# Attention into a token and channel mixer on one core: the order of the first batch, and where transposes find their PSUM banks

## The chip, the cores and the metric

The kernel runs on one NeuronCore of a Trainium2 chip. A core has engines that run side by side, each with its own queue, worked in order: TensorE (PE, matrix products, with its weight loads shown apart as PEld), VectorE (DVE), ScalarE (ACT) and GpSimd (POOL), and SyncE (SP), which here only issues transfers. Matrix products land in PSUM, from which VectorE and ScalarE copy results to SBUF. The metric is the device time of one execution in microseconds. Before the change the median of 6 runs is 382.45 us, from 381.56 to 384.02.

## The reference

Attention with squared ReLU in place of softmax, for 8 batch entries, 12 heads, 448 positions and 64 columns a head; then a mixer over tokens and one over channels:

```python
scores = scale * np.matmul(q, k.transpose(0, 1, 3, 2))
attn = np.maximum(scores, 0.0) ** 2 / S
x = np.matmul(attn, v)             # heads side by side: (8, 448, 768)
h = np.maximum(xt @ w_tok1, 0.0) @ w_tok2          # xt: x with tokens last
u = x + h.transpose(0, 2, 1)
h2 = np.maximum(u @ w_ch1, 0.0) @ w_ch2
out = u + h2
```

The token weights are 448 x 256 and 256 x 448, the channel weights 768 x 1536 and 1536 x 768. Inputs and output are float32; the kernel computes in bfloat16 with float32 sums.

## The kernel before

**Groups.** The 96 heads are worked in 24 groups of four heads; three groups make up one batch entry. A group goes through these steps, each a Python function that appends instructions to the engines' queues.

- `load_four(i)` (L73) loads q, k and v of four heads, two transfers for each tensor, on POOL's queue. They turn float32 into bfloat16 on the way. Only k of group 0 comes over the SP and ScalarE queues as float32 and is cast. Each POOL transfer also waits for the transfer eight places before it, since eight semaphores go round.
- `transposes(i)` (L128): 56 small PE transposes put q and k with the head dimension on the partitions, in two halves r; each half is one PSUM bank (128 x 896 bfloat16) and is copied to the SBUF tile `qkT` (L152).
- `scores(i, c)` (L157): seven tiles c of a group. Four products into a pair of banks, then ReLU on ScalarE (L172) into a tile `at`. `square` (L176) squares finished tiles on VectorE and can keep the last one back.
- `values(i, cs)` (L181) multiplies the tiles with v and sums into `acc_ps`, two banks; `values_out` (L200) scales both halves into `xT`, on VectorE, or with `split` the second half on ScalarE.
- `x_back` (L222) transposes x for the token product: for the first six groups on PE, into one bank, with a copy to `x_sb`; later by transfers on SP's queue.
- `token1` (L252) is the first token product, with ReLU on ScalarE (L265) into `r_sb`; `token2` (L268) is the second; its two halves `h_ps` are added to `xT` into `uT_sb` on VectorE (L289). `u_back` then sends u back transposed through SP's queue.
- `channel1` (L315): one unit is six products of 128 x 448 and a ReLU, 12 units a batch entry. `channel2` (L353): twelve products of 128 x 384 and an addition.

**PSUM.** The pool `ps_att` has two pairs of banks, which the score tiles take in turn; `ps_acc` has one pair, for `acc_ps` and several others; `ps_mm` has two single banks, taken in turn. The 8 banks are all given away. A tile of a pool can be written again once every reader of the tile before it in that place is done. The framework finds all waits from the tiles that instructions read and write.

**Order.** The order is written out by hand, in three stretches. The first (L439 to L464) is a loop over groups 0 to 2 and, in each, over the seven score tiles; the work of the group before (its last three value tiles, its token products) is put between them. The second (L467 to L495) is group 3 written out, with the first channel products (`channel1_begin` and `channel1_end`, which split two units so that the last third of u can come late). The third (L497 on) is a loop over the other groups. In it `fill(share)` takes channel units from a queue: each call adds a share of `rate` to a credit, and units are taken while the credit is positive, or at least `least` of them.

In the first two stretches the transposes are called with `early=True`: each half takes a bank of `ps_mm` of its own, and ScalarE copies half 0, VectorE half 1. The same banks serve `x_back`, `token1` and `token2`. The transposes of group i+1 are put behind score tile 3 of group i. In the third stretch they use the pair of `ps_acc`, and VectorE copies both halves.

Of the kernel before, what the change touches and what calls it, by code (L numbers as in the profile page):

```python
# [9 lines left out]
FP32 = mybir.dt.float32  # L10
BF16 = mybir.dt.bfloat16
# [5 lines left out]
def kernel(  # L17
# [52 lines left out]

    raws = {}
    k_first = consts.tile([128, 2, QC, D], FP32, name="k_first")
    def load_four(i):  # L73
        b, d = divmod(i, DB)
        tiles = []
        for name, src in (("q", q), ("k", k), ("v", v)):
            t = raw.tile([128, 2, QC, D], BF16, name=f"{name}_raw")
            for r in range(2):
                h0 = 4 * d + 2 * r
                eng, dst = nc.gpsimd, t  # L80
                if i == 0 and name == "k":
                    eng, dst = (nc.sync, nc.scalar)[r], k_first
                eng.dma_start(  # L83
                    out=dst[64 * r : 64 * (r + 1)].rearrange("p g c d -> p g (c d)"),
                    in_=src[b, h0 : h0 + 2].rearrange("g (p c) d -> p g (c d)", c=QC),
                )
            if i == 0 and name == "k":
                nc.scalar.copy(t[:, 0], k_first[:, 0])
                nc.vector.tensor_copy(t[:, 1], k_first[:, 1])
            tiles.append(t)  # L90
        raws[i] = tiles

    def load_wt1():
        w = moe_w_tok1.rearrange("(p c) j -> c p j", c=QC)
# [30 lines left out]

    qkT, at2, squares, accs = {}, {}, [], {}

    def transposes(i, early=False):  # L128
        sb = attn.tile([128, 2, 2, S], BF16, name="qkT")
        if early:  # L130
            parts = [ps_mm.tile([128, 1024], BF16, tag="bank", name="qkT_ps1") for r in range(2)]
        else:
            both = ps_acc.tile([128, 2, 1024], BF16, tag="acc", name="qkT_ps")
            parts = [both[:, r] for r in range(2)]
        for w in (1, 0) if i == 0 else (0, 1):
            src = raws[i][w]
            for c in range(QC):
                at = w * S + c * 64
                for r in range(2):
                    h = slice(64 * r, 64 * (r + 1))  # L140
                    for g in range(2):
                        nc.tensor.matmul(  # L142
                            parts[r][64 * g : 64 * (g + 1), at : at + 64],
                            lhsT=src[h, g, c, :],
                            rhs=ident[h, h],
                            is_transpose=True,
                            start=True,
                            stop=True,
                            skip_group_check=True,
                        )  # L150
        for r in range(2):
            (nc.scalar.copy if early and r == 0 else nc.vector.tensor_copy)(  # L152
                sb[:, r].rearrange("n w t -> n (w t)"), parts[r][:, : 2 * S]
            )
        qkT[i] = sb

# [22 lines left out]
            nc.vector.tensor_tensor(out=at, in0=at, in1=at, op=ALU.mult)  # L179

    def values(i, cs):  # L181
        v_raw = raws[i][2]
        if i not in accs:
            accs[i] = ps_acc.tile([128, 2, 512], FP32, tag="acc", name="acc_ps")
        ps = accs[i]
        for c in cs:
            at = at2.pop((i, c))
            for r in range(2):
                for g in range(2):
                    h = slice(64 * r, 64 * (r + 1))  # L190
                    nc.tensor.matmul(  # L191
                        ps[64 * g : 64 * (g + 1), r, :S],
                        lhsT=v_raw[h, g, c, :],
                        rhs=at[h, g, :],
                        start=(c == 0),
                        stop=(c == QC - 1),
                        skip_group_check=True,
                    )

    def values_out(i, split=False):  # L200
        b, d = divmod(i, DB)
        ps = accs.pop(i)
        raws.pop(i)
        for r in range(2):
            if split and r == 1:
                nc.scalar.activation(
# [13 lines left out]
    XDMA = 6  # L220
# [44 lines left out]
        nc.scalar.activation(r1, ps, AF.Relu)  # L265
        r1_tiles[i] = r1

    def token2(i, early=False):  # L268
        b, d = divmod(i, DB)
        if d == 0 and b % 2 == 0:  # L270
            uT_tiles[b // 2] = mix.tile([128, NP, 2 * S], BF16, name="uT_sb")
        r1 = r1_tiles.pop(i)
        off = (b % 2) * S
        if early:
            parts = [ps_mm.tile([128, 512], FP32, tag="bank", name="h_ps1") for r in range(2)]
        else:
            both = ps_acc.tile([128, 2, 512], FP32, tag="acc", name="h_ps")
            parts = [both[:, r] for r in range(2)]
        for r in range(2):
            for j in range(JC):  # L280
                nc.tensor.matmul(  # L281
                    parts[r][:, :S],
                    lhsT=r1[:, j, r * 128 : (r + 1) * 128],
                    rhs=wt2[:, j, :],
                    start=(j == 0),
                    stop=(j == JC - 1),
                )
        for r in range(2):
            nc.vector.tensor_tensor(  # L289
                out=uT_tiles[b // 2][:, 2 * d + r, off : off + S],  # L290
                in0=parts[r][:, :S],
                in1=xT[b % 2][:, 2 * d + r, :S],
                op=ALU.add,
            )
        u_back(i)


    r2_tiles, u_tiles, out_tiles = {}, {}, {}
# [127 lines left out]
        nc.vector.memset(xT[i][:, :, S:], 0.0)  # L426
    nc.vector.memset(wt1[:, 3, :], 0.0)
    make_identity(nc, ident)
    load_four(0)
    load_four(1)  # L430
    load_wt1()
    load_four(2)
    load_wt2()
    load_four(3)
    load_wc1(0, 2)
    order_wt2()


    transposes(0, early=True)  # L439
    for i in range(DB):  # L440
        for c in range(QC):
            scores(i, c)
            square(keep=1)
            if c < 3 and i > 0:
                values(i - 1, (4 + c,))
                if c == 2:
                    values_out(i - 1)
            if c == 0 and i > 1:
                token2(i - 2, early=True)
            if c == 3:  # L450
                transposes(i + 1, early=True)
            if c == 4 and i > 0:
                x_back(i - 1)
            if c == 5:
                values(i, (0, 1))
            if c == 6:
                if i > 0:
                    token1(i - 1)
                values(i, (2, 3))
        if i == 1:  # L460
            load_four(4)
# [12 lines left out]
    scores(i, 1)  # L474
    token1(i - 1)
    square(keep=1)
    first = channel1_begin()
    scores(i, 2)
    token2(i - 1, early=True)
    square(keep=1)  # L480
    channel1_end(first)
    scores(i, 3)
    transposes(i + 1, early=True)
    square(keep=1)
    scores(i, 4)
    channel_work(0)
    queue.pop(0)[1]()
    square(keep=1)
    scores(i, 5)
    scores(i, 6)  # L490
    square(keep=1)
    queue.pop(0)[1]()
# [3 lines left out]

    rate[0] = len(queue) * C1 / DB  # L497
    for i in range(DB + 1, ND + 2):
        if i == 2 * DB + 1:
            rate[0] = (EC * C1 + NT * C2) / DB  # L500
        if i < ND:
# [4 lines left out]
            values_out(i - 1)  # L506
        if i < ND:
            scores(i, 2)
        if i - 1 < XDMA:
            fill(1 / 3, least=1)  # L510
        if 0 <= i - 1 < ND:
            x_back(i - 1)
# [4 lines left out]
        if i == 4:  # L517
            load_wc2(1, 2)
        square()
        if i - 1 >= XDMA:  # L520
            fill(1 / 3)
        if i < ND:
            scores(i, 3)
# [1 line left out]
        if i + 1 < ND:  # L525
            transposes(i + 1)
        square()
        fill(2 / 9)
        if 0 <= i - 1 < ND:
            token1(i - 1)  # L530
        fill(1 / 9, least=1)
        if i < ND:
            scores(i, 5)
            scores(i, 6)
# [38 lines left out]
```

## Time and profile before

| quantity | value |
|---|---|
| median of 6 runs | 382.45 us (381.56 to 384.02) |
| the profiled execution | 381.56 us, span 379.8 us |
| PE busy | 363.1 us, 96% of the span |
| VectorE busy | 205.5 us, 54% |
| ScalarE busy | 213.9 us, 56% |
| GpSimd busy | 98.3 us, 26% |
| PE busy from 0 to 10 us, 10 to 20, 20 to 30, 30 to 40 | 6.42, 7.18, 7.95, 8.27 us |
| ReLU of one score tile (L172) | 0.92 us, 168 times |
| square of one tile (L179) | 0.63 us, 168 times |
| mean granted TensorE clock | 0.999 |

The span is the time from the first to the last instruction of the profiled execution. "Busy" is the time in which an engine has an instruction at work. In a view of waits, a line names the engine and line that waited, what it waited for, the total, the number of times and the longest wait, all in us. In the timeline a line has the start, the length, the engine, the line, the operation, output and input, the count, and in brackets the idle time before it with what ended it. A strip cuts the span in 40 slices, with the busy share of each in tenths.

### The profile page before, as it was taken

What the parts mean: (1) busy time and instruction counts of PE and PEld (TensorE: products, weight loads), DVE (VectorE), ACT (ScalarE), POOL (GpSimd) and SP (SyncE); (2) the same over time, 40 slices, a digit from 0 to 9 for tenths busy, and PEclk for the clock granted to TensorE, in tenths of its full rate; (3) what the DMA queues carried; (4) which work ended last, traced back from release to release, by engine and by line L of the source; (5) the groups of instructions that cost most, each with busy time, mean ns of one, the idle gap of its engine ahead of it and who ended that gap; (6) DMA issues with size and microseconds to landing.
All of it is one profiled execution on the core that took longest, in us unless ns stands there. A gap on an engine that the chain in (4) does not pass through costs nothing.

```text
span 379.8 us, 10027 instructions
## 1 busy us (share of the span) xinstructions
PE 363.1 (96%) x4281; PEld 200.0 (53%) x4281; DVE 205.5 (54%) x373; ACT 213.9 (56%) x297; POOL 98.3 (26%) x176
## 2 busy tenths in 40 slices
PE   6768899999999999999999999999999999999995
PEld 2444455554565555555555655555545654555563
DVE  1795577864486575465555665556654755121022
ACT  3985887867545447754676247654676455411400
POOL 9976244330412303303303303313300000000000
PEclk9999999999999999999999999999999999999999
DMA  8999999974658868648746688498551343223024
GB/s 155 128 198 179 191 203 190 167 99 73 92 140 148 164 117 135 99 70 157 128 76 93 115 169 145 44 115 157 116 84 24 83 109 87 42 65 89 2 56 110
DMA packets 72013, 43.82 MB, mean 115 GB/s; under 512 B 46048, under 2 KB 68512, under 8 KB 71968
## 3 DMA queue, kind: packets, MB, share of 16 engines
q0 software_dynamic: 24416, 21.47, 39.5%
q1 hardware_dynamic: 47248, 21.28, 28.0%
q8 instruction: 33, 0.54, 0.6%
q10 hardware_dynamic: 304, 0.43, 0.4%
q14 instruction: 12, 0.10, 0.1%
HBM read 43.38 MB, written 11.01 MB: 143 GB/s over the span
## 4 chain that ended last, share of the span: by engine, by line
PE 87%; ACT 5%; DVE 4%; issue 2%; DMA 1%; POOL 0%; POOLq 0%; ACTq 0%
PE m_ps L361 29%; PE m_ps L322 28%; PE sc_ps L163 9%; PE acc_ps L191 8%; PE t_ps L257 5%; PE h_ps L281 4%; ACT at L172 4%; PE qkT_ps L142 2%; DVE at L179 2%; DMA q_raw<-in_q_dram 1%; PE x_ps L235 1%; DVE uT_sb L289 1%; ACT qkT L152 1%; PE m_ps L340 1%; DVE qkT L152 1%
## 5 line engine op out<-in xcount | busy, mean ns | idle before, releaser
L172 ACT ACTIVATE at<-sc_ps 128x896 bf16<-128x896 f32 x168 | 144.9, 923 | 60.3 <-PE sc_ps L163 60.3
L322 PE MATMUL m_ps<-uT_sb,wc 128*128 128x448 bf16 x564 | 115.3, 353 | 0.7 <-DVE qkT L152 0.7
L361 PE MATMUL m_ps<-wc,r_sb 128*128 128x384 bf16 x672 | 115.2, 326 | 0.0
L179 DVE TENSOR_TENSOR at<-at 128x896 bf16<-128x896 bf16 x168 | 98.0, 625 | 6.3 <-ACT at L172 6.2
L361 PEld LDWEIGHTS <-r_sb 128*128 128x128 bf16 x672 | 64.3, 98 | 45.8 <-issue 4.1
L329 ACT ACTIVATE r_sb<-m_ps 128x448 bf16<-128x448 f32 x94 | 51.3, 545 | 58.8 <-PE m_ps L322 58.3
L322 PEld LDWEIGHTS <-wc 128*128 128x128 bf16 x564 | 53.2, 98 | 50.2 <-issue 5.0
L368 DVE TENSOR_TENSOR out_sb<-m_ps,u_sb 128x384 f32<-128x384 f32 x56 | 31.1, 556 | 58.8 <-PE m_ps L361 58.8
L163 PE MATMUL sc_ps<-qkT 64*64 64x448 bf16 x672 | 54.0, 368 | 5.0 <-ACT at L172 3.6
L289 DVE TENSOR_TENSOR uT_sb<-h_ps,xT 128x448 bf16<-128x448 f32 x48 | 27.7, 620 | 50.5 <-PE h_ps L281 50.4
L210 DVE TENSOR_SCALAR xT<-acc_ps 128x448 bf16<-128x448 f32 x47 | 27.2, 620 | 29.1 <-PE acc_ps L191 29.1
L515 POOL COPY gate<-x_sb 1x1 bf16<-1x1 bf16 x14 | 3.4, 242 | 145.2 <-DMA x_sb<-xT 145.2
L191 PE MATMUL acc_ps<-at,v_raw 64*64 64x448 bf16 x672 | 38.3, 353 | 0.1
L83 POOL DMA_DIRECT2D q_raw<-in_q_dram x48 | 28.9, 611 | 27.1 <-DMA wc<-in_moe_w_ch_dram 23.1
L152 DVE COPY qkT<-qkT_ps 128x896 bf16<-128x896 bf16 x43 | 25.1, 620 | 19.3 <-PE qkT_ps L142 18.0
L163 PEld LDWEIGHTS <-qkT 64*64 64x64 bf16 x672 | 16.2, 106 | 33.6 <-issue 29.7
L83 POOL DMA_DIRECT2D v_raw<-in_v_dram x48 | 29.5, 641 | 2.9 <-PE h_ps L281 1.6
L83 POOL DMA_DIRECT2D k_raw<-in_k_dram x46 | 28.0, 628 | 0.8 <-DMA k_raw<-in_k_dram 0.4
L191 PEld LDWEIGHTS <-v_raw 64*64 64x64 bf16 x672 | 20.6, 107 | 12.0 <-issue 1.8
L257 PE MATMUL t_ps<-x_sb,wt 128*128 128x256 bf16 x192 | 24.9, 273 | 0.8 <-ACT x_sb L246 0.8
L265 ACT ACTIVATE r_sb<-t_ps 128x512 bf16<-128x512 f32 x24 | 14.3, 598 | 19.3 <-PE t_ps L257 19.3
L281 PE MATMUL h_ps<-wt,r_sb 128*128 128x448 bf16 x96 | 22.3, 355 | 0.0
(36 smaller groups left out, 106.4 us busy)
## 6 DMA issues: line engine op xcount, KB each, us to landing
out_dram<-out_sb SPq DMA_DIRECT2D x54, 192.0 KB, 2.8
q_raw<-in_q_dram POOLq DMA_DIRECT2D x48, 112.0 KB, 4.0
v_raw<-in_v_dram POOLq DMA_DIRECT2D x48, 112.0 KB, 4.6
k_raw<-in_k_dram POOLq DMA_DIRECT2D x46, 112.0 KB, 4.4
wc<-in_moe_w_ch_dram POOLq DMA_DIRECT2D x4, 1152.0 KB, 14.5
u_sb<-uT_sb SPq DMA_TRANSPOSE x48, 3.2
x_sb<-xT SPq DMA_TRANSPOSE x36, 2.5
k_first<-in_k_dram SPq DMA_DIRECT2D x1, 224.0 KB, 3.5
```

What stands on the lines that cost most here:

```text
L83: eng.dma_start(out=dst[64 * r : 64 * (r + 1)].rearrange("p g c d -> p g (c d)"), in_=src[b, h0 : h0 + 2].rearrange("g (p c) d -> p g (c d ...
L152: (nc.scalar.copy if early and r == 0 else nc.vector.tensor_copy)(sb[:, r].rearrange("n w t -> n (w t)"), parts[r][:, : 2 * S])
L163: nc.tensor.matmul(ps[64 * r : 64 * (r + 1), g, :S], lhsT=sb[h, r, 1, c * 64 : (c + 1) * 64], rhs=sb[h, r, 0, :], start=True, stop=True, s ...
L172: nc.scalar.activation(at, ps[:, :, :S], AF.Relu)
L179: nc.vector.tensor_tensor(out=at, in0=at, in1=at, op=ALU.mult)
L191: nc.tensor.matmul(ps[64 * g : 64 * (g + 1), r, :S], lhsT=v_raw[h, g, c, :], rhs=at[h, g, :], start=(c == 0), stop=(c == QC - 1), skip_gro ...
L257: nc.tensor.matmul(ps[:, j, :], lhsT=wt1[:, c, j * 128 : (j + 1) * 128], rhs=x_sb[:, :, c, :], start=(c == 0), stop=(c == 3),)
L281: nc.tensor.matmul(parts[r][:, :S], lhsT=r1[:, j, r * 128 : (r + 1) * 128], rhs=wt2[:, j, :], start=(j == 0), stop=(j == JC - 1),)
L289: nc.vector.tensor_tensor(out=uT_tiles[b // 2][:, 2 * d + r, off : off + S], in0=parts[r][:, :S], in1=xT[b % 2][:, 2 * d + r, :S], op=ALU.add,
L322: nc.tensor.matmul(ps[:, :S], lhsT=wc1[:, g, e * 128 : (e + 1) * 128], rhs=uT[:, g, off : off + S], start=(g == 0), stop=(g == CC - 1),)
L329: nc.scalar.activation(r2[:, e, off : off + S], ps[:, :S], AF.Relu)
L361: nc.tensor.matmul(ps[:, :HN], lhsT=r2[:, e, t * 128 : (t + 1) * 128], rhs=wc2[:, e, cols], start=(e == 0), stop=(e == EC - 1),)
```

## The change

Five edits, all before or in the third stretch's first three rounds.

1. **Transposes.** `transposes(i, place, split)` takes one tile of two banks from the pool that it is told, for both halves. Group 0 uses `ps_acc`, groups 1 to 4 `ps_att`, where they take a turn among the score tiles. With `split` ScalarE copies half 0 and VectorE half 1 (groups 0, 2, 3, 4); without it VectorE copies both (group 1, and all later ones). For groups 2 and 3 the transposes stand behind score tile 5 of the group before, for group 4 behind tile 4.
2. **Token work.** `x_back` and `token1` of the group before move forward, from tiles 4 and 6 to tiles 3 and 4. `token2` is issued in two halves, behind tiles 0 and 1. `values_out` is split between VectorE and ScalarE in the first stretch too.
3. **Group 3** is written out in another order: scores stand ahead of `channel1_begin`, `token2` and `channel1_end`.
4. **Loads** are issued by tensor: q and k of groups 1 to 3 ahead of their v, and the reorder copies of the second token weights (`order_wt2`, on POOL) ahead of the first half of the channel weights.
5. **Fill.** In the rounds of groups 4 to 6 the shares of `fill` change from 1/3, 2/9, 1/9, 1/3 to 1/3, 0, 1/3, 1/3.

```diff
-    def transposes(i, early=False):
+    def transposes(i, place="acc", split=False):
         sb = attn.tile([128, 2, 2, S], BF16, name="qkT")
-        if early:
-            parts = [ps_mm.tile([128, 1024], BF16, tag="bank", name="qkT_ps1") for r in range(2)]
-        else:
-            both = ps_acc.tile([128, 2, 1024], BF16, tag="acc", name="qkT_ps")
-            parts = [both[:, r] for r in range(2)]
+        pool = {"acc": ps_acc, "att": ps_att}[place]
+        ps = pool.tile([128, 2, 1024], BF16, tag=place, name="qkT_ps")
...
         for r in range(2):
-            (nc.scalar.copy if early and r == 0 else nc.vector.tensor_copy)(
-                sb[:, r].rearrange("n w t -> n (w t)"), parts[r][:, : 2 * S]
+            (nc.scalar.copy if split and r == 0 else nc.vector.tensor_copy)(
+                sb[:, r].rearrange("n w t -> n (w t)"), ps[:, r, : 2 * S]
             )
...
-    def token2(i, early=False):
+    def token2(i, early=False, rs=(0, 1)):
...
-        for r in range(2):
+        for r in rs:
...
-        u_back(i)
+        if 1 in rs:
+            u_back(i)
...
-    load_four(0)
-    load_four(1)
+    load_four(0, "kqv")
+    load_four(1, "qk")
     load_wt1()
-    load_four(2)
+    load_four(2, "qk")
+    load_four(1, "v")
     load_wt2()
-    load_four(3)
+    load_four(2, "v")
+    load_four(3, "qk")
+    order_wt2()
     load_wc1(0, 2)
-    order_wt2()
-
-
-    transposes(0, early=True)
+    load_four(3, "v")
+
+
+    transposes(0, "acc", split=True)
     for i in range(DB):
         for c in range(QC):
             scores(i, c)
...
             if c < 3 and i > 0:
                 values(i - 1, (4 + c,))
                 if c == 2:
-                    values_out(i - 1)
-            if c == 0 and i > 1:
-                token2(i - 2, early=True)
-            if c == 3:
-                transposes(i + 1, early=True)
+                    values_out(i - 1, split=True)
+            if c in (0, 1) and i > 1:
+                token2(i - 2, early=True, rs=(c,))
+            if c == 3 and i == 0:
+                transposes(1, "att")
+            if c == 3 and i > 0:
+                x_back(i - 1)
             if c == 4 and i > 0:
-                x_back(i - 1)
+                token1(i - 1)
             if c == 5:
+                if i > 0:
+                    transposes(i + 1, "att", split=True)
                 values(i, (0, 1))
             if c == 6:
-                if i > 0:
-                    token1(i - 1)
                 values(i, (2, 3))
...
     token1(i - 1)
     square(keep=1)
+    scores(i, 2)
     first = channel1_begin()
-    scores(i, 2)
+    square(keep=1)
+    scores(i, 3)
     token2(i - 1, early=True)
     square(keep=1)
+    scores(i, 4)
     channel1_end(first)
-    scores(i, 3)
-    transposes(i + 1, early=True)
     square(keep=1)
-    scores(i, 4)
+    transposes(i + 1, "att", split=True)
     channel_work(0)
+    scores(i, 5)
+    square(keep=1)
     queue.pop(0)[1]()
-    square(keep=1)
-    scores(i, 5)
     scores(i, 6)
...
+        slow = i <= 2 * DB
...
-        if i - 1 < XDMA:
+        if slow:
             fill(1 / 3, least=1)
...
-        fill(2 / 9)
+        if not slow:
+            fill(2 / 9)
         if 0 <= i - 1 < ND:
             token1(i - 1)
-        fill(1 / 9, least=1)
+        fill(1 / 3 if slow else 1 / 9, least=1)
```

## The prediction

> **What bounds the kernel now.** I read the engine strips first, then the busy time by stage, then the waits of the first 80 us, then the timeline of that stretch.
>
> ```profile
> PE   6768899999999999999999999999999999999995
> ...
> DVE  1795577864486575465555665556654755121022
> ACT  3985887867545447754676247654676455411400
> ```
>
> TensorE is full from the eighth slice (each 9.5 us) to the last; before that it has holes.
>
> ```profile
> 10.00:20.00 10.00, 7.18 (x183) 3.91 (x179) 8.24 (x15) 10.00 (x13) 9.66 (x17) 1.00 0.99 131
> 20.00:30.00 10.00, 7.95 (x160) 4.61 (x159) 9.67 (x16) 8.38 (x12) 6.55 (x10) 1.00 1.26 199
> ...
> 50.00:60.00 10.00, 9.50 (x154) 5.35 (x142) 7.57 (x15) 7.99 (x11) 5.01 (x9) 1.00 1.20 207
> ...
> 80.00:100.00 20.00, 20.00 (x265) 11.00 (x264) 9.80 (x19) 13.68 (x21) 5.97 (x12) 1.00 0.44 68
> ```
>
> The columns after the length are PE, weight loads, VectorE, ScalarE, GpSimd. From 80 us PE never idles, so everything there only shifts. From 10 to 20 us ScalarE is busy all the time, from 20 to 30 us VectorE nearly so: the first batch is bounded by those two, and by how their in-order queues hang together. All that the change can do is move the instant at which PE becomes full (77.4 us, the channel product after group 6's values).
>
> ```profile
> ACT at L172 <- PE sc_ps L163: 5.8, 11, 1.2
> ...
> PE sc_ps L163 <- ACT at L172: 3.6, 10, 0.6
> ...
> PE x_ps L235 <- DVE qkT L152: 3.2, 2, 1.6
> ...
> ACT xT L206 <- DVE xT L210: 1.3, 1, 1.3
> ```
>
> The first two lines are ScalarE and PE waiting for each other over two pairs of banks. The third is a wait that the change removes: x_back's transposes need a bank that the VectorE copy of qkT still reads. The last shows what two engines do that read halves of one PSUM tile: ScalarE's half starts when VectorE's is done. The timeline gives the durations:
>
> ```profile
> 12.83 5.81 ACT L172 ACTIVATE at<-sc_ps 128x896 bf16<-128x896 f32 x7
> ...
> 13.83 0.44 PE L163 MATMUL sc_ps<-qkT 64*64 64x448 bf16 x4 [0.28 <-ACT at L172]
> ...
> 17.26 0.41 PE L142 MATMUL qkT_ps<-ident,q_raw 64*64 64x64 bf16 x26
> ...
> 18.42 1.02 ACT L152 COPY qkT<-qkT_ps 128x896 bf16<-128x896 bf16 x1
> ...
> 19.19 0.62 DVE L152 COPY qkT<-qkT_ps 128x896 bf16<-128x896 bf16 x1
> ...
> 19.86 0.61 PE L235 MATMUL x_ps<-ident,xT 128*128 128x128 bf16 x8 [1.60 <-DVE qkT L152]
> ...
> 20.51 0.69 DVE L248 COPY x_sb<-x_ps 128x1024 bf16<-128x1024 bf16 x1 [0.17 <-PE x_ps L235]
> ...
> 21.29 1.05 PE L257 MATMUL t_ps<-x_sb,wt 128*128 128x256 bf16 x8
> ...
> 22.45 0.60 ACT L265 ACTIVATE r_sb<-t_ps 128x512 bf16<-128x512 f32 x1
> ...
> 32.04 0.62 DVE L210 TENSOR_SCALAR xT<-acc_ps 128x448 bf16<-128x448 f32 x1 [0.48 <-PE acc_ps L191]
> ...
> 32.70 0.54 ACT L206 ACTIVATE xT<-acc_ps 128x448 bf16<-128x448 f32 x1 [1.31 <-DVE xT L210]
> ```
>
> From these and their neighbours, start to start: ReLU to the next ScalarE instruction 0.81 (seven in 5.81, the last 0.92 long); ReLU to the score that reuses its bank pair 1.00 (12.83 to 13.83); score to ReLU 0.43 (20.40 to 20.84); ReLU to square 0.95 (8.82 to 9.77); a VectorE instruction to the next 0.55, to a dependent PE or ScalarE instruction 0.67; half a qkT copy on ScalarE to the next 0.80, to its dependent 0.93; xT half on ScalarE 0.44; a set of transposes 0.62 (about 1.0 before 13 us); x_ps to x_sb 0.65, x_sb to t_ps 0.77, t_ps to r_sb 1.17, t_ps to the next PE work 0.97, r_sb to h_ps 0.69, h_ps to its add 0.61.
>
> **The change, walked through the queues.** (g,c) is score tile c of group g. I follow the new order of each in-order queue and name the ScalarE start of each tile, old one in brackets.
>
> Group 0. One qkT_ps tile now holds both halves, so VectorE's half waits for ScalarE's: 7.22 + 0.93 = 8.15, the r=1 scores at 8.83 instead of beside the first. (0,0) starts at about 9.20 (8.82): +0.37. Transposes(1) now take a turn in the two score bank pairs. The ReLU of (0,2), 10.82, frees theirs at 11.82; they end at 12.8; two VectorE copies (0.55 + 0.67) free the pair at 14.1, so (0,5) starts at 14.55 (13.64). ScalarE saves one copy (0.80) and idles 1.0 and 0.3. (0,6) 15.36 (14.45), (1,0) 16.17 (15.26): +0.91.
>
> Group 1. (1,2) 17.79. values_out is now split: VectorE takes its half behind the square of (1,1), at 16.98 + 0.95 + 0.55 = 18.48; ScalarE's half, which stands ahead of (1,3) in its queue, waits to 19.14 (0.54 idle), then 0.44: (1,3) 19.58 (17.69). x_ps no longer waits for the qkT copy, but for xT's second half: second part 19.75, x_sb 20.2, t_ps 20.97 (21.29): the removed wait of 1.6 returns 0.3. r_sb now stands between (1,4) at 20.58 and (1,5): at 22.14, after 0.75 idle, (1,5) at 22.69 (20.84). Transposes(2) end at 22.77, ScalarE's copy 23.50, VectorE's half only after it, 24.43; pair free at 25.10; (2,0) at 25.53 (23.08): +2.45.
>
> Group 2. VectorE is now the chain: square (1,6) 25.53, uT half 26.11, square (2,0) 26.66, uT half 27.21, square (2,1) 27.75, xT half 28.30. ScalarE's xT half at 28.96 after 0.87 idle: (2,3) 29.40 (26.06). x_ps second part 29.56, x_sb 30.0, t_ps 30.78 (29.62), r_sb 31.93, (2,5) 32.48 (29.17), copy 33.29, (2,6) 34.09 (29.98). The last values of group 2: square 35.33, PE 36.0 (31.61): +4.4. Splitting token2 itself is free: both halves are ready when reached.
>
> Group 3. h_ps 36.5, x_ps 37.77, t_ps 39.51 (35.12). Here scores moved ahead of waits do help: PE idled 0.33 + 0.82 + 0.52 + 0.58 + 0.26 us from 32 to 44. (3,2), channel1_begin, (3,3), token2(2), (3,4) follow without a gap; uT's second half 43.55, channel1_end from 44.23, its ReLU 45.0, transposes(4) 44.9 to 45.4, copies 45.81 and 46.75, pair free 47.42, so (3,6) 47.87; a channel unit each side; values(3) start at 49.4 (46.3): +3.1.
>
> Groups 4 to 6. fill now gives 1/3, 1/3 and 1/3, the second after token1 and the third behind token2, where before PE idled 0.5 of each 10 us. Credit arithmetic (1/3 of the rate is 8/9 of a unit, least=1) gives three units, three, two, as before; the third fills the hole for groups 4 and 5, 0.5 each, and group 6 has none left for it: -1.0. token1 straight behind the transposes costs about nothing: x_ps to t_ps needs 0.65 + 0.77 = 1.42, and four PE steps of 1.5 cover it (group 6 has this order already: 69.38 to 70.90). If that cover went, 0.3 a group would show. After that the order on all engines is unchanged.
>
> Loads. POOL issues one in about 0.6 us. v of group 1 moves behind wt1's seven and four q, k issues: 12.4 instead of 6.3, +4.4 landing, 18.0, read at 22.8. wt2_nat is issued at 13.6 and lands at 19.1; the two reorder copies (2.14) then stand before the channel weights, which go at 21.5 instead of 19.31 and land 12.3 later, 33.8, for a first reader at 40.6 (35.9 before). The load eight places on waits for them (33.8 instead of 31.86), so the second half goes at about 38 and lands at 50.3; its reader, the third unit of group 4, is at 57 (52.4). Nothing; if the chains above were not late, the smallest slack left would be 2 us. SP's queue is the same.
>
> Sum: +3.1 - 1.0 = **+2.1 us**. The profiled execution took 381.56 with a span of 379.8, 0.9 below the median of 382.45; the step makes 383.7 of it, and 384.5 of the median. Bounds of what no row shows: the early transposes at 0.62 instead of 1.0 give back 0.4; the ends of the walk, +0.37 each for a late half, lie within 1 us either side; the fill is worth 0.5 to 1.5.
>
> The page "PSUM — Partial Sum Buffer" of the Trainium skill (PSUM bank collisions raise a hardware error) says that ScalarE and VectorE may read different banks at once; the halves of acc_ps and qkT_ps are different banks. The 1.31 us wait at L206 stands on just such halves, and in the built order VectorE's half of the split qkT copies waits for ScalarE: the wait is made by tile, not by bank. By the page's rule the split copies would overlap and the sum would be that of the faster rival below.
>
> The page "TensorE: Matmul & The Clock Gate" (The HAM clock gate) lets a sparse PE run at half clock. The granted clock here is 1.00 in all rows to 360 us, though a score set took 0.59 at 9.8 us and 0.38 from 14.6; by the page, sparser early work could keep the slow pace longer.
>
> **The rivals.** *Faster*: the halves are read side by side. Then these go: 0.37 (group 0), 0.98 (group 1's ScalarE wait and work before (1,3)), 0.42 ((2,0)), 1.31 (group 2), 0.55 ((3,6)), 3.6 in all: 3.1 - 3.6 - 1.0 = -1.5, 381.0. For: they are in different banks. Against: the L206 row. It decides if the second half starts less than 0.3 after the first. *No change*: the holes that I see on ScalarE are absorbed, because group 3 has 2.5 us of PE idle and the walk takes back only 1.3 of it (4.4 to 3.1); with all of it and 1.5 from the fill the sum is 4.4 - 2.5 - 1.5 = +0.4, 382.9. Against: t_ps to channel1_end is a chain that keeps its length. *Much slower*: the early PE pace (scores 0.6, transposes 1.0) lasts through group 2; three transposes and some twelve scores on the chain, 0.38 and 0.2 each, +3.5 on top: 388. Against: the pace changed by 14 us before.
>
> **How the numbers follow.** Forecast 0.65 (383.6 to 386.3), no change 0.15, faster 0.1, much slower 0.1. The range leaves out the faster rival and the end of the much slower one: 382.9 to 387. 0.3% is 1.15 us, about what a measurement can tell. Slower: 0.65 + 0.1, less the forecast's low tail, 0.73; the same 0.17; faster 0.1.
>
> **What would show it.** In the changed profile: ScalarE's xT copy waiting about 0.5 and 0.9 for VectorE in groups 1 and 2; VectorE's qkT copies waiting for ScalarE; no wait of x_ps for a qkT copy; a ReLU wait on scores after each set of transposes; (2,0) near 25.5; values of group 3 near 49; PE full in groups 4 and 5; unchanged order from the first all-full slice. I am wrong if group 2's token1 starts before 30 us, or if scores never wait for a qkT copy.

## The result and the profile after

The changed kernel takes **384.68 us** (median of 21 runs, 383.26 to 385.44) against 382.83 us for the kernel before (42 runs, 381.31 to 384.32). The ratio is 1.0045, with a 95% interval of 1.0033 to 1.0057: slower by 1.7 us (382.83 x 0.0045). The forecast was 384.5, from 382.9 to 387.0. One run of one kernel further down took 863.59 us, in a slow state, and is left out of all times given here.

The profiled execution has a span of 383.2 us and took 384.98 us. That is 3.4 us above the profiled execution before (381.56), twice the step of the medians: the one before is 1.3 below its median, the one after 0.3 above. Start times of the two profiles, set side by side below, carry this difference. The strips and stages that the prediction read look like this now:

```profile
PE   6786899999999999999999999999999999999995
...
DVE  1666578863575665556555665555744755121022
ACT  3876788776554347654676446764576455411400
```

```profile
10.00:20.00 10.00, 7.40 (x124) 3.64 (x123) 7.41 (x13) 8.00 (x11) 8.75 (x16) 1.00 1.05 140
20.00:30.00 10.00, 7.96 (x132) 3.67 (x129) 6.52 (x12) 7.85 (x10) 6.22 (x10) 0.83 1.01 160
...
50.00:60.00 10.00, 10.00 (x161) 5.49 (x163) 7.51 (x14) 8.36 (x13) 3.28 (x6) 1.00 1.21 186
```

ScalarE was busy for 10.0 of the 10 us from 10 to 20; it is at 8.00 now. VectorE was at 9.67 of the 10 us from 20 to 30; it is at 6.52. Neither is full any more and the stretch is longer: the bound has become a chain that goes through both, one after the other. From 50 to 60 us PE is busy all the time, where it was at 9.50. And one number is new: the granted clock of the second line is 0.83.

The waits of the first 82 us:

```profile
DVE qkT L148 <- ACT qkT L148: 8.6, 4, 2.8
ACT at L168 <- PE sc_ps L159: 5.8, 13, 1.3
...
ACT xT L201 <- DVE xT L205: 3.0, 3, 2.0
...
PE sc_ps L159 <- ACT at L168: 2.0, 6, 0.6
PE sc_ps L159 <- DVE qkT L148: 2.0, 3, 0.8
```

The first line is the second half of a split qkT copy waiting for the first, in all four places. The third is the same in xT's split. The last line is new: three score tiles wait for a qkT copy. Two of them, (0,5) and (3,6), wait for the copy to free their banks. The third, (2,0), at 26.45, reads the qkT that is being copied and would wait for both halves in any bank. The wait of x_ps for a qkT copy (3.2 us in two waits) is gone.

The chain of waits, in order of time (start, length, engine, tile, line; the lines named "issue" between these, 0.02 to 0.27 us each, are left out):

```profile
18.57 0.63 DVE at L175
19.19 0.55 DVE xT L205
19.76 0.55 ACT xT L201
20.36 0.46 PE x_ps L230 x4
20.84 0.70 DVE x_sb L243
21.59 1.88 PE t_ps L252 x8
23.49 0.60 ACT r_sb L260
24.08 0.48 ACT at L168
24.84 0.91 ACT qkT L148
25.77 0.64 DVE qkT L148
26.45 0.38 PE sc_ps L159 x4
```

This is group 1 as the prediction walked it: square, first half of xT, second half on ScalarE, x_back, token1, its ReLU, the score tile behind it, one half of the qkT copy, then the other, then the first score of group 2. One step took far longer than it should: t_ps takes 1.03 to 1.05 us in the kernel before and 1.88 here.

How the walk stands to the trace, by the start of an instruction:

| step | before | forecast | after |
|---|---|---|---|
| ReLU of (0,0) | 8.82 | 9.20 | 9.12 |
| ReLU of (0,5) | 13.64 | 14.55 | 14.57 |
| ReLU of (1,0) | 15.26 | 16.17 | 16.81 |
| token1 of group 0 | 21.29 | 20.97 | 21.59 |
| ReLU of (2,0) | 23.08 | 25.53 | 26.88 |
| token1 of group 1 | 29.62 | 30.78 | 32.11 |
| token1 of group 2 | 35.12 | 39.51 | 40.67 |
| values of group 3 | 46.12 | 49.4 | 50.83 |
| values of group 4 | 56.35 | 59.1 | 60.13 |
| values of group 6 | 75.69 | 78.0 | 79.15 |

(The forecasts of the last two rows are 49.4 plus the old distances less the forecast savings of 0.5 a round.) The walk holds step by step, with two slips of 0.6 and 0.7 us on the way to (2,0). Both are matmuls at a slower pace: in this execution a score set took 0.59 us until 16.8 us and again from 20.7 to 23.4.

### The profile page after: what moved, and what is told of

The parts are those of the page before. It is cut to its first block, busy times and chain, and to the rows that moved or that the text cites. A ratio compares the mean times of both kernels' runs of the same rounds, so it can differ in the third digit from the quotient of the medians.

```text
span 383.2 us, 10020 instructions
## 1 busy us (share of the span) xinstructions
PE 365.8 (95%) x4281; PEld 199.5 (52%) x4281; DVE 204.2 (53%) x372; ACT 214.9 (56%) x298; POOL 97.7 (25%) x176
## 4 chain that ended last, share of the span: by engine, by line
PE 90%; ACT 4%; DVE 3%; DMA 1%; issue 1%; ACTq 0%
PE m_ps L357 29%; PE m_ps L318 28%; PE sc_ps L159 10%; PE acc_ps L187 8%; PE t_ps L252 6%; PE h_ps L276 5%; PE qkT_ps L138 3%; ACT at L168 2%; DMA k_first<-in_k_dram 1%; DVE qkT L148 1%; ACT qkT L148 1%; DVE uT_sb L284 1%; PE x_ps L230 1%; DVE at L175 1%; PE m_ps L336 1%
## 5 line engine op out<-in xcount | busy, mean ns | idle before, releaser
L159 PE MATMUL sc_ps<-qkT 64*64 64x448 bf16 x672 | 55.0, 374 | 5.3 <-ACT at L168 2.0
L205 DVE TENSOR_SCALAR xT<-acc_ps 128x448 bf16<-128x448 f32 x45 | 26.1, 620 | 29.8 <-PE acc_ps L187 29.8
L148 DVE COPY qkT<-qkT_ps 128x896 bf16<-128x896 bf16 x44 | 25.6, 620 | 25.5 <-PE qkT_ps L138 16.8
L252 PE MATMUL t_ps<-x_sb,wt 128*128 128x256 bf16 x192 | 25.9, 279 | 2.0 <-ACT x_sb L241 0.8
L252 PEld LDWEIGHTS <-wt 128*128 128x128 bf16 x192 | 18.7, 99 | 8.0 <-issue 2.4
```

The costliest lines, as they stand in the source:

```text
L148: (nc.scalar.copy if split and r == 0 else nc.vector.tensor_copy)(sb[:, r].rearrange("n w t -> n (w t)"), ps[:, r, : 2 * S])
L159: nc.tensor.matmul(ps[64 * r : 64 * (r + 1), g, :S], lhsT=sb[h, r, 1, c * 64 : (c + 1) * 64], rhs=sb[h, r, 0, :], start=True, stop=True, s ...
L252: nc.tensor.matmul(ps[:, j, :], lhsT=wt1[:, c, j * 128 : (j + 1) * 128], rhs=x_sb[:, :, c, :], start=(c == 0), stop=(c == 3),)
```

## The experiments

Each kernel was timed together with the kernel before. A time "against the kernel before" is the ratio of its runs, with the interval, in us of 382.8. "The changed kernel" stands at +1.7 on that scale. A difference between two such kernels is uncertain by about 1 us, by their intervals.

### Do the new fill shares alone bring what was said?

The kernel before, with edit 5 alone:

```diff
+        slow = i <= 2 * DB
...
-        fill(2 / 9)
+        if not slow:
+            fill(2 / 9)
         if 0 <= i - 1 < ND:
             token1(i - 1)
-        fill(1 / 9, least=1)
+        fill(1 / 3 if slow else 1 / 9, least=1)
```

> The kernel before with the new fill shares alone. Forecast's step: the third channel unit of groups 4 and 5 fills a hole of 0.5 us each, -1.0 us. From the changed kernel's own profile (9.30 us from values to values in place of 10.07 and 10.23): -1.7. Rival, that the hole only moves to another wait (ScalarE's ReLUs, or token1 behind the transposes): 0.

Measured: 381.81 us against 382.79, ratio 0.9967 (0.9951 to 0.9983), -1.3 us. Values to values now takes 9.3 us in the rounds of groups 4 and 5 (47.47, 56.79, 66.09) where it took 10.23 and 10.24. So the rounds give 0.93 each, 1.9 in all. In this profiled execution 1.75 of it is lost again a little later:

```profile
77.47 3.18 SPq L228 DMA_TRANSPOSE x_sb<-xT  x2
...
85.50 1.03 PE L257 MATMUL t_ps<-x_sb,wt 128*128 128x256 bf16 x8 [1.75 <-DMA x_sb<-xT]
```

Group 6 is the first whose x goes back by transfers. Issued at 77.5, they are awaited until 85.5, among the loads and the u transposes, and PE, which is earlier now, waits for them. In the profile of the kernel before the same token1 started at 84.11 and did not wait.

### Are the loads free?

The kernel before, with edit 4 alone:

```diff
-    load_four(0)
-    load_four(1)
+    load_four(0, "kqv")
+    load_four(1, "qk")
     load_wt1()
-    load_four(2)
-    load_wt2()
-    load_four(3)
-    load_wc1(0, 2)
-    order_wt2()
+    load_four(2, "qk")
+    load_four(1, "v")
+    load_wt2()
+    load_four(2, "v")
+    load_four(3, "qk")
+    order_wt2()
+    load_wc1(0, 2)
+    load_four(3, "v")
```

> The kernel before with the new order of loads alone. Forecast's step: 0, within 0.4 us, since every load lands before its reader. Rival, that q and k first feed the transposes sooner: below -1 us; rival, that later weights or v hold somebody up: above +1 us.

Measured: 383.65 us, ratio 1.0022 (1.0001 to 1.0043): +0.8 us, and its interval reaches from nothing to 1.6. The trace of one execution shows a wait that would make it:

```profile
53.95 1.31 PE L320 MATMUL m_ps<-uT_sb,wc 128*128 128x448 bf16 x6 [1.72 <-DMA wc<-in_moe_w_ch_dram]
```

The second half of the channel weights was issued at 39.16 (35.24 before), behind the first half, which now waits for the reorder copies on POOL. It arrived only after the third channel unit of group 4 was due (at 52.4 in the kernel before). The forecast had it issued at about 38 and landed at 50.3; it was issued at 39.16, and the unit that needed it started at 53.95. The same edit taken out of the changed kernel:

> The changed kernel with the loads in their old order. The new order alone, in the kernel before, made a channel unit of group 4 wait 1.7 us for the second half of the channel weights. In the changed kernel that unit comes later: 0 within 0.4 against the changed kernel by the forecast; -0.8 if the loads cost the same in either order of work.

Measured: 384.15 us, ratio 1.0040 (1.0021 to 1.0058), against 1.0045 for the changed kernel: the loads cost nothing there, within 0.9 us. In the changed kernel the third unit comes later, at 58.50, and in its profile the second half goes at 35.78. So the edit is free in one order of work and not, at least in the profiled execution, in the other.

### Is ScalarE's wait for its half of xT what costs?

The changed kernel, with xT of groups 0 and 1 on VectorE alone:

```diff
-                    values_out(i - 1, split=True)
+                    values_out(i - 1)
```

> The changed kernel with values_out of groups 0 and 1 on VectorE alone, as before (group 2's stays split). If ScalarE's wait for its half of xT is what costs (2.3 us in the forecast's list): -2 us against the changed kernel, so level with the kernel before. If the chain runs through the second half of xT to x_back and token1, whichever engine makes it: 0 within 0.4, still about +1.9 against the kernel before. If the slow TensorE clock makes the loss: 0 as well, or noise of the clock.

Measured: 384.29 us, ratio 1.0047 (1.0024 to 1.0069): no difference from the changed kernel. ScalarE no longer waits in groups 1 and 2, and the chain goes the same way with VectorE's second half in place of ScalarE's: token1 of groups 0, 1 and 2 starts at 21.82, 32.21 and 40.77, against 21.59, 32.11 and 40.67. The waits of 0.42 and 0.56 us that the profile shows at L201 (the prediction had 0.54 and 0.87) were off the path: taking them away changes nothing while the second half of xT comes no sooner.

### Are the serial copies what costs?

The changed kernel, with both halves of the qkT copies of groups 2 to 4 on VectorE:

```diff
-                    transposes(i + 1, "att", split=True)
+                    transposes(i + 1, "att")
...
-    transposes(i + 1, "att", split=True)
+    transposes(i + 1, "att")
     channel_work(0)
```

> The changed kernel with both qkT copies of groups 2 to 4 on VectorE, so that no half waits for ScalarE and ScalarE has 0.8 us less in each of these groups; VectorE has 0.55 more. If the serial pair of copies in a shared score bank pair makes the loss: the pair is free about 0.9 us sooner in each of groups 2 and 3 and 0.5 in group 4, -1.5 us against the changed kernel, near +0.4 against the kernel before. If the clock makes it: no change, +1.9.

Measured: 384.28 us, ratio 1.0025 (1.0002 to 1.0048), so 0.8 us less than the changed kernel, with intervals that overlap. The profiles are plainer: values of group 3 start at 49.43 instead of 50.83, though both profiled executions have the same granted clock of 0.72 from 20 to 26 us. One engine doing both halves is done sooner than two in a row.

The next kernel gives the transposes of the changed order two single-bank tiles again, as before. The calls for groups 0 to 4 name `"mm"` as the place, and group 1's copies are split as well. So two things change: the halves are in tiles of their own, and the transposes no longer take a turn among the score tiles.

```diff
-        pool = {"acc": ps_acc, "att": ps_att}[place]
-        ps = pool.tile([128, 2, 1024], BF16, tag=place, name="qkT_ps")
+        if place == "mm":
+            parts = [ps_mm.tile([128, 1024], BF16, tag="bank", name="qkT_ps1") for r in range(2)]
+        else:
+            ps = ps_acc.tile([128, 2, 1024], BF16, tag="acc", name="qkT_ps")
+            parts = [ps[:, r] for r in range(2)]
```

> The changed kernel with the transposes of groups 0 to 4 in two single-bank tiles as before (halves copied side by side, no turn taken among the score tiles), in the new places. If the shared, serial banks make the loss: group 0 gives back 0.37 + 0.54, groups 1 to 3 about 0.4 each by earlier score tiles, less 0.6 a group where the transposes wait for token1's bank: -1.5 to -2 us against the changed kernel, level with the kernel before or 0.5 above. If the other moves (x_back, token1, split xT) or the clock make it: at most -0.5, still +1.3.

Measured: 382.64 us, ratio 1.0010 (0.9986 to 1.0034): 1.3 us less than the changed kernel, level with the kernel before (the ratio holds one run of 387.32; the medians are 382.64 and 382.74). The two copies run side by side:

```profile
22.93 0.62 DVE L151 COPY qkT<-qkT_ps 128x896 bf16<-128x896 bf16 x1 [2.29 <-PE qkT_ps L141]
22.94 0.91 ACT L151 COPY qkT<-qkT_ps 128x896 bf16<-128x896 bf16 x1 [0.21 <-PE qkT_ps L141]
```

In the changed kernel the same pair runs in a row:

```profile
24.84 0.90 ACT L148 COPY qkT<-qkT_ps 128x896 bf16<-128x896 bf16 x1
...
25.77 0.62 DVE L148 COPY qkT<-qkT_ps 128x896 bf16<-128x896 bf16 x1 [2.82 <-ACT qkT L148]
```

### Is the bank edit bad by itself?

The kernel before in its own order, with edit 1 in the old places alone:

```diff
-    transposes(0, early=True)
+    transposes(0, "acc", split=True)
...
             if c == 3:
-                transposes(i + 1, early=True)
+                transposes(i + 1, "att", split=i > 0)
...
-    transposes(i + 1, early=True)
+    transposes(i + 1, "att", split=True)
```

> The kernel before in its own order, with only the bank edit: one tile for both halves, in the accumulators' pair for group 0 and in the score pairs for groups 1 to 4. By the walk: +0.9 at the end of group 0, another 0.8 to 1.1 in each of groups 1 and 2 (the score behind the transposes waits for both copies), 0.5 in group 3, of which later PE idle absorbs one: +2 us against the kernel before, and no wait of x_ps for a qkT copy. If the bank edit is harmless or helps by the removed waits of 1.6 us: 0 to -2.

Measured: 383.17 us, ratio 1.0009 (0.9992 to 1.0027), +0.3 us in place of the +2 expected. Group 0 loses what was said, and after it nothing is added: token1 of groups 0, 1 and 2 starts 1.2, 1.2 and 1.0 us later than before, values of group 3 1.15. (The granted clock of this execution is 0.61 from 7 to 14 us and 0.60 from 14 to 20, against 1.00 in the profile before, so not all of the first 1.2 need be the banks'.) In each of groups 1 and 2 the wait of 1.60 us of x_ps for the qkT copy is gone, and a score tile waits 0.57 for the copies instead, behind which VectorE gets to x_sb only at 21.73 (20.51): the period of a group stays at 8.4 us (22.46 to 30.83; 21.29 to 29.62 before). The edit swaps one wait for another of the same worth.

### Which of the moved places costs?

The changed kernel, with x_back and token1 back behind tiles 4 and 6:

```diff
-            if c == 3 and i > 0:
-                x_back(i - 1)
             if c == 4 and i > 0:
-                token1(i - 1)
+                x_back(i - 1)
...
             if c == 6:
+                if i > 0:
+                    token1(i - 1)
                 values(i, (2, 3))
```

> The changed kernel with x_back and token1 back behind score tiles 4 and 6; transposes stay behind tile 5 in the shared banks. In the walk token1's ReLU then stands behind (1,5) on ScalarE and no longer makes it wait 0.75 for x_sb, and scores no longer stand behind x_ps on TensorE: (2,0) at 24.35 in place of 25.53, as much again in group 2: -2 us against the changed kernel, level with the kernel before or 0.5 below. If the place of the transposes or the banks make the loss: 0 to -0.5, still +1.3 or more.

Measured: 383.13 us, ratio 1.0009 (0.9989 to 1.0028): 1.4 us less than the changed kernel, the expected 2 within the intervals. ScalarE runs three ReLUs on end where it waited for token1:

```profile
19.59 0.54 ACT L201 ACTIVATE xT<-acc_ps 128x448 bf16<-128x448 f32 x1 [0.42 <-DVE xT L205]
20.03 2.53 ACT L168 ACTIVATE at<-sc_ps 128x896 bf16<-128x896 f32 x3
```

In the changed kernel token1's ReLU stands between them and keeps (1,5) waiting:

```profile
21.37 0.92 ACT L168 ACTIVATE at<-sc_ps 128x896 bf16<-128x896 f32 x1 [0.26 <-PE sc_ps L159]
...
23.49 0.60 ACT L260 ACTIVATE r_sb<-t_ps 128x512 bf16<-128x512 f32 x1 [1.20 <-PE t_ps L252]
...
24.02 0.92 ACT L168 ACTIVATE at<-sc_ps 128x896 bf16<-128x896 f32 x1
```

Then all three places as before, with the shared banks kept:

```diff
             if c == 3 and i > 0:
-                x_back(i - 1)
+                transposes(i + 1, "att", split=True)
             if c == 4 and i > 0:
-                token1(i - 1)
+                x_back(i - 1)
             if c == 5:
-                if i > 0:
-                    transposes(i + 1, "att", split=True)
                 values(i, (0, 1))
             if c == 6:
+                if i > 0:
+                    token1(i - 1)
                 values(i, (2, 3))
```

> The changed kernel with transposes, x_back and token1 all in their old places (tiles 3, 4, 6) and the shared banks kept. If the measured parts add up (banks +0.4, fill -1.3, order of group 3 -1.1) and the places are the whole rest: -2.0 us against the kernel before, -3.7 against the changed kernel. If the split xT and token2 or the loads carry some of the rest: between -1 and 0 against the kernel before.

Measured: 383.78 us, ratio 1.0051 (1.0019 to 1.0082). Two of the twelve runs, 388.67 and 388.93, make the interval wide; the median is 0.5 us above that of the kernel before in the same rounds (383.32). The parts do not add up: -2.0 was the sum. Against the profile of the kernel with the bank edit alone, token1 of group 0 is 0.9 us later (23.35 against 22.46), of group 1 1.9, of group 2 3.1. The profile has ScalarE's half of xT ahead of (1,3) and of the qkT copy here, so that the copy starts at 20.59 instead of 19.72, which was free in the changed kernel's places. About half of the further delay, 1.1 us, lies between token1 of group 1 and of group 2, from 32 to 39 us, where the granted clock of this execution is below 1. How much the split token2 adds was not tried by itself.

### Is it the clock?

The changed kernel, with 12 idle transposes on PE ahead of x_back's in groups 0 and 1:

```diff
+        for k in range(12 if i < 2 else 0):
+            nc.tensor.matmul(
+                ps[:, 0, :128], lhsT=ident, rhs=ident, is_transpose=True,
+                start=True, stop=True, skip_group_check=True,
+            )
         for r in range(2):
```

> The changed kernel with 12 idle transposes of the identity ahead of x_back's own in groups 0 and 1, into the same bank, where TensorE waits 0.8 to 1.1 us anyway; they compute nothing that is kept. If the sparser TensorE and its halved clock carry much of the loss: the granted clock from 20 to 26 us stays at 1.00 and the time falls by 0.5 to 1 us. If the chain of waits on ScalarE and VectorE makes it: 0, or +0.3 where the clock is slow already.

Measured: 385.24 us (median of five runs), ratio 1.0078 (1.0049 to 1.0107): no gain. A loss against the changed kernel is not clear: two of the five runs took 2.6 and 3.4 us more than their span, where it is 1.7 to 1.9 in all other runs, and the spans average 383.3 against 382.7. In the profiled execution the clock did what was wanted. These are the stages of this kernel, and then of the changed one; the number before the last two of a line is the granted clock:

```profile
20.00:26.00 6.00, 4.44 (x106) 2.54 (x106) 4.12 (x6) 5.09 (x8) 5.40 (x8) 1.00 0.83 110
26.00:32.00 6.00, 4.99 (x60) 2.75 (x62) 5.33 (x10) 4.72 (x7) 1.66 (x3) 1.00 1.21 202
```

```profile
20.00:26.00 6.00, 5.18 (x100) 2.79 (x98) 2.60 (x5) 4.54 (x7) 6.00 (x10) 0.72 0.91 127
26.00:32.00 6.00, 3.88 (x44) 1.53 (x44) 5.38 (x11) 4.96 (x7) 1.54 (x4) 1.00 1.20 206
```

In its profile token1 of group 2 starts at 39.47 and the values of group 3 at 49.63, which is the forecast's walk (39.51 and 49.4) to 0.2 us: without slow matmuls in the middle, the chain alone makes the 3.5 us that this execution is late there against the profile before. The mean granted clock over a run is 0.990 on average in this kernel and in the kernel before beside it, 0.986 in the changed one. So the clock is a little lower in the changed kernel, but holding it up buys nothing that the times show; whether the idle transposes cost as much as they saved can't be told from these runs.

The granted clock of a row does not tell the whole pace. In the profile of the xT kernel above it is 1.00 from 7 to 32 us, and yet a score set takes 0.59 us until 21 and t_ps 1.83; its values of group 3 start at 50.92, as late as in the changed kernel (50.83). The durations of the matmuls are the surer sign.

### Two versions that go below both kernels

The kernel before with edit 5 and with edit 3's order of group 3, the transposes in their own two banks:

```diff
-    first = channel1_begin()
     scores(i, 2)
+    first = channel1_begin()
+    square(keep=1)
+    scores(i, 3)
     token2(i - 1, early=True)
     square(keep=1)
+    scores(i, 4)
     channel1_end(first)
-    scores(i, 3)
-    transposes(i + 1, early=True)
     square(keep=1)
-    scores(i, 4)
+    transposes(i + 1, early=True)
     channel_work(0)
-    queue.pop(0)[1]()
-    square(keep=1)
     scores(i, 5)
+    square(keep=1)
+    queue.pop(0)[1]()
     scores(i, 6)
```

> The kernel before with the new fill shares and the new order of group 3 (scores ahead of the first channel products and token2), transposes in their own banks. The order takes back the 1.3 us of TensorE idle that the walk found for it in group 3: -2.3 us against the kernel before (fill alone measured -1.3). If that idle is only moved: -1.3, as with the fill alone.

Measured: 380.38 us, ratio 0.9939 (0.9920 to 0.9958), **-2.3 us**, as expected. From token1 of group 2 to the values of group 3 it takes 10.26 us (36.37 to 46.63); with the fill alone 11.00 (36.47 to 47.47). That is 0.7 of the 1.1 us between the two kernels' times.

On top of it, the first batch's token work later instead of earlier:

```diff
-            if c == 0 and i > 1:
-                token2(i - 2, early=True)
+            if c == 0 and i > 1:
+                token1(i - 2)
+            if c == 2 and i > 1:
+                token2(i - 2, early=True)
...
-            if c == 4 and i > 0:
-                x_back(i - 1)
             if c == 5:
+                if i > 0:
+                    x_back(i - 1)
                 values(i, (0, 1))
             if c == 6:
-                if i > 0:
+                if i == 2:
                     token1(i - 1)
```

> The kernel before with the new fill and order of group 3, and in the first batch the opposite of the changed places: x_back of a group later (behind tile 5), token1 of group 0 behind the first score tile of group 2 and its token2 behind the third. Then ScalarE has the next score tile ready where it waited for x_ps and token1 (0.8 and 0.8 us in group 1): -1 us on top of the -2.3 of those two edits, -3.3 against the kernel before. If ScalarE's waits there are not on the path: -2.3; if VectorE or the two single banks bind: above -2.

Measured: 380.65 us, ratio 0.9947 (0.9926 to 0.9969): the same as without it. Its values of group 1 end 2.9 us earlier (22.97 against 25.85 for the start of the last four), and token1 of group 1 starts at 30.76 against 30.87: the lead is gone within group 2. In the profiled execution token2 of group 0 (h_ps) waits 0.76 us for POOL's reorder copies of the second token weights, which end at 24.33. Then the transposes wait where the single banks are not free, since uT's adds now come just ahead of them:

```profile
26.46 0.22 PE L142 MATMUL qkT_ps<-ident,q_raw 64*64 64x64 bf16 x2 [1.04 <-DVE uT_sb L289]
```

## Why the prediction was right

**The size and the side.** 384.5 was forecast from the median, 384.68 came; in 1.0045 the step is +1.7 us, forecast +2.1. That the sum is this close is in part luck: its two terms, the walk and the fill, were both too small and cancel.

**The walk, +3.1.** Its steps came as named: the late half of group 0, the score that waits for the banks of transposes(1), token1's ReLU in front of (1,5), the copies in a row, VectorE's chain in group 2. In the kernel with idle transposes, whose matmuls are not slow in the middle, it measures 3.5 (49.63 less 46.12; the prediction's +3.1 counts from 46.3). In the changed kernel's own profile it is 4.7, 1.2 more: 0.3 of that is there ahead of token1 of group 0 (21.25 against 21.59), and the rest is t_ps, 1.04 us in the one and 1.88 in the other. All these differences are taken from one profile before, and that execution is an early one (see the loads below). The forecast held the slow pace to the first 14 us and made its lasting a rival of 1 in 10, worth 3.5; it is rather a part of many executions, and smaller. (t_ps of group 0 took 1.83 to 1.88 us in the profiles of the changed kernel, the xT kernel, the one-engine copies and the old loads.)

**The fill, -1.0.** The term was mis-sized: 0.93 a round, 1.9 in all, measured in the fill kernel and in the changed one (50.83, 60.13, 69.43). The step counted only PE's idle time of 0.5 in 10 us. The chain of waits of the kernel before had booked 0.31 and 0.70 us of issuing in that place as well, and a channel unit between token2 and the next scores covers both.

**The rival "faster"** was priced by adding up waits. Its three terms for the qkT copies (0.37, 0.42 and 0.55) make 1.34, and the kernel with own banks, where these copies run side by side, gained 1.3. The other two, 0.98 and 1.31, were ScalarE's waits and work for xT. The xT kernel took both off ScalarE and gained nothing; reading xT's halves side by side was not tried. The rival's condition was not met: nothing ran side by side in the changed kernel. **The rival "no change"** fell: in the profile group 3 took back 0.8 (token1 of group 2 is 5.55 late, values of group 3 4.71); the walk had said 1.3, this rival 2.5.

**The loads, nothing.** Right for the changed kernel, not as a statement on the edit: alone it made PE wait 1.72 us for the channel weights in its profiled execution. (The 18.0 for the landing of v of group 1 is not 12.4 + 4.4, but nothing hangs on it with a reader at 22.8.) The edit also takes away a wait that the profile of the kernel before does not show. There the reorder copies of the second token weights ran from 20.66 to 22.80, just ahead of token2 of group 0 at 23.15. In the fill kernel, the same up to that point, their transfer came later, and token2 waited 1.4 us in all:

```profile
22.97 1.68 POOL L106 COPY wt<-wt_nat 128x448 bf16<-128x448 bf16 x2 [1.98 <-DMA wt_nat<-in_moe_w_tok_dram]
23.89 0.35 PE L281 MATMUL h_ps<-wt,r_sb 128*128 128x448 bf16 x1 [0.94 <-POOL wt L106]
24.70 0.73 PE L281 MATMUL h_ps<-wt,r_sb 128*128 128x448 bf16 x3 [0.46 <-POOL wt L106]
```

The kernel with the fill and the order of group 3 shows the same (0.87 and 0.46). In these two, token1 of group 2 starts at 36.47 and 36.37, where the profile before has 35.12. So that profile is an early one, by 1.3 us at this place, and what the changed kernel loses, read against it, may be too large by as much. In every profile with the new order of loads the copies end by 22.8, and none of them shows this wait (in most of them token2 comes later, too). How often it comes in the kernel before is open.

**The two pages of the Trainium skill.** "PSUM — Partial Sum Buffer" (PSUM bank collisions raise a hardware error) says that ScalarE and VectorE may read different banks at once. The copies at 22.93 and 22.94, from two tiles in two banks, agree. In one tile over two banks the same copies ran in a row, at 24.84 and 25.77: the rule is about banks, the waits that were built are about tiles. "TensorE: Matmul & The Clock Gate" (The HAM clock gate) says that a sparse PE falls to half its clock. The row agrees in this execution: granted 0.72 from 20 to 26 us, where t_ps took 1.88 us instead of 1.03 a group later. That this decides the time, the kernel with idle transposes did not bear out.

**What was left open.** One execution's profile of the changed kernel has a gap of 0.47 us inside token1 of group 5 that no view explains. The parts measured one by one do not make the whole: -1.3 (fill), -1.1 (order of group 3), +0.3 (banks) and +0.8 (loads) make -1.3, where the changed kernel is at +1.7. Edit 2 is missing from that list; it was not measured alone. But a chain of three kernels brackets it. Fill and order of group 3 stand at -2.3. The kernel with own banks adds edit 2, the loads and the later place of the transposes, and stands 2.7 us higher (1.0010 against 0.9939; 1.5 to 3.9 by the intervals). The changed kernel adds the shared banks, 1.3 more. So the larger part of the loss comes with the early token work and what goes with it, the smaller with the banks. The old places of x_back and token1 gave back 1.4, in the shared banks. How the rest divides between the split token2, the split xT, the loads and the place of the transposes is open, and old places with own banks were not tried together.

## What to carry to other kernels

When several in-order queues feed each other, a wait in the profile is not a price: walk the queues in the new order, step by step, and take the difference at the far end; here that came within half a microsecond of the total, with some luck, while 2.3 us of ScalarE's waits and work at the split xT were worth nothing when they were taken away. Compare more than one profile before trusting such a difference: the same instructions started 1.3 us apart in two executions. A tile over two PSUM banks that two engines copy in halves makes them go one after the other; give each half a tile of its own, or let one engine do both. And instructions moved ahead in one queue (token1's ReLU) stand in front of others that could run sooner: put work early only where its input is there.

## What the runs showed that was not expected

- The granted PE clock differs from execution to execution and falls for some microseconds in the sparse first 39 us, at different places: 0.72 from 20 to 26 us in the changed kernel's profile, 0.61 from 7 to 14 us in that of the bank edit alone, 0.77 from 32 to 39 us in that of the old places, 1.00 throughout in the kernel with the fill and the order of group 3.
- A gain in front meets the transfers behind: in two profiled executions of the faster versions PE waited 1.75 and 2.0 us for x_sb of group 6, the first that comes by transfer.
- The shared banks, which cost 1.3 us in the changed order, cost 0.3 in the old one (a difference of about 1 us, as large as its uncertainty): they remove a wait of 1.6 us a group there and put another in its place.
